# The last block's output path: VectorE 32x32 turns and 128-byte rows for five of six chunks, in place of TensorE turns

## The chip, the cores and the metric

The kernel runs on one core of one Trainium2 chip. The metric is the device time of one execution in microseconds (us), the median of several runs.

## The reference

Sigmoid attention over 4 batches, 12 heads, 448 tokens and head size 64 gives 1792 rows of 768 columns. Two mixture-of-experts layers follow. The first sends a token through its expert only where a skip score is above zero, and adds its result to the token. The second sends every token through the expert with the highest cosine score. Only the second matters here:

```python
h = np.maximum(x[mask] @ w1[e], 0.0)      # 768 -> 1024
out[mask] = gate_w[mask, None] * (h @ w2[e])   # 1024 -> 768, scaled per token
```

The output is float32, 1792 x 768, in token order.

## The kernel before

The kernel works on one batch of 448 tokens at a time, and holds activations turned: 128 of the 768 columns on the partitions, 448 tokens along the free axis. In the second layer each batch has one expert that most of its tokens chose. That expert runs densely over the whole batch ("block", `dense`). The few tokens with another expert are gathered into an "item" of 32 places, run through their own expert, and scattered to the output by row number with an indirect DMA on GpSimd's queue.

There are four such blocks, j = 0 to 3, in an order that the routing sets at run time. A block loops over f = 0 to 7 (128 hidden units each). `h(f)` makes hidden units with 18 matmuls (every product is three matmuls, from operands split into a high and a low part), and `y(f - 1)` adds the previous units' share to six PSUM tiles `YS[0]` to `YS[5]`, one per chunk of 128 output columns, 18 matmuls again. Hooks `sub(0)` to `sub(15)` between them run small steps of other work at fixed places. The order of instructions on each engine is the order in which the code writes them. Waits between engines, and between DMAs and engines, are put in by the framework from the tiles and tensors that an instruction reads and writes, unless the code declares two instructions independent (`declare_no_dep`).

The result of a block is in PSUM with columns on the partitions, and the output wants tokens on rows, so it has to be turned and scaled by each token's gate.

Blocks 0 to 2 do it in `finish`. VectorE turns each chunk in squares of 32x32 (L1421) from PSUM into the tile `STG`; the access pattern places token 14r + k at column 32k + r beforehand, so that partition 32g + r then holds the tokens 14r to 14r + 13, and of each chunk the 32 columns of group g. GpSimd multiplies by the gate (L1423) into the tile `ROW`; the gate comes in that layout from `gate_tokens`, which makes it in two steps among the hooks: a VectorE product (L1403) and one small matmul (L1410) with a copy (L1412). Four DMAs on SyncE's queue (L1430) then store it, one for each group g of 32 partitions, in rows of 32 floats, 128 bytes. These stores are issued at hook 2 of the next block.

The last block does it in `finish_last`, because no later block hides it. Its last two steps f = 6 and 7 are ordered chunk by chunk. ScalarE or VectorE copies a finished chunk to `STG` (L1450, L1448, and for the last chunk half each, L1445 and L1446). TensorE transposes it in four pieces of 112 tokens (L1394) into PSUM places that have come free. ScalarE (L1467) and VectorE (L1465) scale a token row each by the gate, which lies on the partitions here. Three stores (L1470) follow: chunks 0 to 2 on SyncE's queue, chunks 3 and 4 on ScalarE's queue, chunk 5 on SyncE's. Between the second store and the work for chunk 5 comes `it.early`: the item's second product into `YS[0]`, 64 matmuls (L1031), its gate (L1045) and its scatter (L1068).

The stores of `finish_last` are declared independent of each other only where they are on different queues:

```python
for other in STORES:
    if other.ins.engine != st.ins.engine:
        tc.declare_no_dep(st.ins, other.ins, reason="disjoint columns")
```

The four stores of `finish` have no such declaration.

Of the kernel before, what the change touches and what calls it, by code (L numbers as in the profile page):

```python
# [14 lines left out]
ALU = mybir.AluOpType  # L15
# [6 lines left out]
def sigmoid_attention_moe_moe_kernel(  # L22
# [1359 lines left out]
    e = expert_of(0)  # L1382
    b = nc.values_load(K["pb"][0:1, 8:9], engines=[ENG.SP], min_val=0, max_val=B - 1)

    def scaled(g, c, d, n, t):
        row = ROW[:P, c * DM + d * 128 : c * DM + (d + n) * 128]
        if (c + (n == 2)) % 2:
            nc.vector.tensor_scalar(row, t, g[:, c : c + 1], None, op0=ALU.mult)
        else:
            nc.scalar.activation(row, t, AF.Copy, scale=g[:, c : c + 1])  # L1390

    def turn_out(t, w, c, d):
        o = d * S + c * P
        nc.tensor.transpose(t[:P, w : w + 128], STG[:, o : o + P], ident)  # L1394

    def gate_tokens(j, box):

        a = SEL[:P, :128]

        def ready():  # L1400
            g = dense_gate(R2, j)
            four = [P, 4, C, 8]
            nc.vector.tensor_tensor(  # L1403
                a.rearrange("p (g c r) -> p g c r", g=4, r=8), g.unsqueeze(1).unsqueeze(3).to_broadcast(four),
                K["seg"][:P].unsqueeze(1).unsqueeze(1).to_broadcast(four), op=ALU.mult,
            )

        def turned():
            ps = bank("ps_gt")
            nc.tensor.matmul(ps[:, :NK], lhsT=a, rhs=K["off"][:P], start=True, stop=True)  # L1410
            t = box["gt"] = sm.tile([128, NK], F32, tag="gtt", name="gtt", bufs=1)
            nc.vector.tensor_copy(t, ps[:, :NK])  # L1412

        return {3: ready, 8 if j else 9: turned}

    def finish(j, b, gt):

        turned = STG.rearrange("p (d k f) -> p d k f", d=ND, f=32)
        ready = ROW[:, : ND * S].rearrange("p (k d f) -> p k d f", d=ND, f=32)
        for d in range(ND):  # L1420
            nc.vector.transpose(turned[:, d], YS[d][:, :S].rearrange("p (r k) -> p k r", k=NK))  # L1421
        for d in range(ND):
            nc.gpsimd.tensor_tensor(  # L1423
                ready[:, :, d], turned[:, d], gt.unsqueeze(2).to_broadcast([128, NK, 32]), op=ALU.mult
            )

        def store():
            to = out.rearrange("(b r k) (d g f) -> b r k d g f", b=B, k=NK, g=4, f=32)
            for g in range(4):
                nc.sync.dma_start(  # L1430
                    to[ds(b, 1), :, :, :, g].rearrange("o r k d f -> r (o k) d f"), ready[32 * g : 32 * g + 32]
                )

        return store

    def finish_last(j, b, it=None):


        place = {0: BANKS + YS[1:3], 3: YS[3:5] + BANKS, 5: [YS[1], YS[2]]}

        def copy(c):
            o = STG[:, c * S : (c + 1) * S]
            if c == ND - 1:
                w = S // 2
                nc.scalar.activation(o[:, :w], YS[c][:, :w], AF.Copy)  # L1445
                nc.vector.tensor_copy(o[:, w:], YS[c][:, w:S])  # L1446
            elif c % 2:
                nc.vector.tensor_copy(o, YS[c][:, :S])  # L1448
            else:
                nc.scalar.activation(o, YS[c][:, :S], AF.Copy)  # L1450

        def turns(d, d0):
            for c in range(C):
                if d0 < 5:
                    turn_out(place[d0][c], (d - d0) * 128, c, d)
                else:
                    turn_out(place[d0][c % 2], c // 2 * 128, c, d)

        def store(g, d0, d1, queue, bq):
            for c in range(C):  # L1460
                row = ROW[:P, c * DM + d0 * 128 : c * DM + d1 * 128]
                n = (d1 - d0) * 128
                t = place[d0][c][:P, :n] if d0 < 5 else place[d0][c % 2][:P, c // 2 * 128 : c // 2 * 128 + 128]
                if c % 2:
                    nc.vector.tensor_scalar(row, t, g[:, c : c + 1], None, op0=ALU.mult)  # L1465
                else:
                    nc.scalar.activation(row, t, AF.Copy, scale=g[:, c : c + 1])  # L1467
            cols = slice(d0 * 128, d1 * 128)
            to = out.rearrange("(b c p) d -> p b c d", c=C, p=P)[:, ds(bq, 1), :, cols]
            st = queue.dma_start(  # L1470
                to.rearrange("p o c d -> p (o c) d"),
                ROW[:P].rearrange("p (c d) -> p c d", d=DM)[:, :, cols],
            )
            for other in STORES:
                if other.ins.engine != st.ins.engine:
                    tc.declare_no_dep(st.ins, other.ins, reason="disjoint columns")
            STORES.append(st)

        def end(yc, rest):
            g = dense_gate(R2, j)  # L1480
            bq = batch_of(j)

            def both(c):
                yc(NF - 2, c)
                yc(NF - 1, c)
                copy(c)

            for c in range(3):
                yc(NF - 2, c)
            rest()  # L1490
            for c in range(3):
                yc(NF - 1, c)
                copy(c)
            both(3)
            for d in range(3):
                turns(d, 0)
            store(g, 0, 3, nc.sync, b)
            both(4)
            turns(3, 3)
            turns(4, 3)  # L1500
            store(g, 3, 5, nc.scalar, bq)
            early = it.early(STORES) if it else None
            both(5)
            turns(5, 5)
            store(g, 5, 6, nc.sync, b)
            if early:
                tc.declare_no_dep(STORES[-1].ins, early, reason="rows of another batch")
                it.late(STORES)

        return end  # L1510
# [7 lines left out]
    for j in range(B):  # L1518
        box = {"e": e}
        last = j == B - 1  # L1520
        if last:
            todo = {}
        else:
            todo = at_subs((3, 5, 7), route2_steps(j + 1, XST[(j + 1) % 2])[:3])
            for n, at in ROUTED.get(j, ()):
                todo = merge(todo, at_subs(at, route2_steps(n, None)[3:]))
            todo = merge(todo, gate_tokens(j, box))
        if j == 0:
            load_unit(v1, v2, e, 1)
            halves()  # L1530
            for f in split_unit(0, FIRST_RAW)[3:]:
                f()
            todo = merge({-0.5: lambda: spread(item_b())}, todo)
        if j == B - 2:
            todo = merge(todo, item_steps(R2, (9, 11, 13)), {13: lambda: likely("single")})
        if pend:
            todo = merge({2: pend}, todo)

        def units2(k):
            u, r = k // 4, k % 4  # L1540
            if r == 0 and u + 2 < NU:
                load_unit(v1, v2, box["e"], u + 2)
            if k == 10 and not last:
                box["n"] = expert_of(j + 1)
                load_unit(v1, v2, box["n"], 0)
            if (u + 1 < NU or not last) and r % 2 == 0:
                for f in split_unit((u + 1) % NU)[:3] if r == 0 else split_unit((u + 1) % NU)[3:]:
                    f()
            if k == 12 and not last:
                load_unit(v1, v2, box["n"], 1)  # L1550

        xs = XST[j % 2]
        if not last:
            dense(xs, beside(units2, todo))
            pend = finish(j, b, box["gt"])
            b, e = nc.values_load(K["pb"][0:1, 9 + j : 10 + j], engines=[ENG.SP], min_val=0, max_val=B - 1), box["n"]
            continue

        def with_item():
            it = Item(1, 0)  # L1560
            at, prep = it.ready(0)
            steps = schedule(merge(todo, at), prep, (5, 5, 7))
            dense(xs, beside(units2, steps), end=finish_last(j, b, it))

        n = 3 * NL[1]
        with tc.If(nc.values_load(R2.LI[0:1, n + 3 : n + 4], min_val=0, max_val=NL[1]) < 1, label="single") as cmp:
            with tc.If(count(R2) > 0) as cmp2:
                with_item()
            with cmp2.Else():
                STORES = []  # L1570
                dense(xs, beside(units2, todo), end=finish_last(j, b))
            with tc.If(nc.values_load(R2.LI[0:1, n + 1 : n + 2], min_val=0, max_val=NL[1]) > 0):
                others(1)
        with cmp.Else():
            STORES = []
            with_item()
# [33 lines left out]
```

## Time and profile before

| | |
|---|---|
| time, median of 3 runs | 552.51 us (551.93 to 552.78) |
| the profiled execution's own time | 553.05 us |
| its span, first to last instruction | 551.2 us |
| TensorE matmul busy | 542.9 us, 98% of the span |
| VectorE busy | 298.4 us, 54% |
| ScalarE busy | 252.4 us, 46% |
| GpSimd busy | 54.8 us, 10% |
| mean granted TensorE clock | 0.999 |

Busy time is an engine's time in instructions, and the span is what the profiler recorded between the first and the last instruction. The profiled execution is one run with its own time, some tenths from the median of the three. Times in the rows below are microseconds from the start of the span, and a duration in ns is marked as such.

### The profile page before, as it was taken

Reading aid. Unit: us, or ns where it says so; the run is one execution under the profiler, and the core shown is the slowest. Engines: PE = TensorE matmul, PEld = TensorE weight load, DVE = VectorE, ACT = ScalarE, POOL = GpSimd, SP = SyncE. Lnnn points to the kernel's source line nnn. Section 1 sums busy time; section 2 is a strip of 40 time slices with the busy share of each in tenths; the row PEclk is TensorE's granted clock in tenths of the full one; section 3 lists DMA queues with packets and bytes.
Section 4 is the critical chain, followed back from the end, with each engine's and each line's share of the span. In section 5 each row is a group of like instructions: output and inputs, shape, how many; then the busy total and the mean of one; then the engine's idle time right before and its main releaser. Section 6 shows DMA issues by size and latency. Waiting matters only on the chain.

```text
span 551.2 us, 10110 instructions
## 1 busy us (share of the span) xinstructions
PE 542.9 (98%) x3663; PEld 425.3 (77%) x3663; DVE 298.4 (54%) x810; ACT 252.4 (46%) x410; POOL 54.8 (10%) x133
## 2 busy tenths in 40 slices
PE   8999999999999999999999999999999999999995
PEld 5464644645389889899869898999899998989984
DVE  3643445237777678674138777694486435543212
ACT  5766676766943365323209462175233421222112
POOL 5010000000000000254000000040003000305000
PEclk9999999999999999999999999999999999999999
DMA  9777666773561513315637106227624731546353
GB/s 179 138 124 135 115 111 112 126 129 83 200 187 50 172 58 120 115 59 160 242 121 283 55 15 241 89 48 171 213 76 103 219 118 59 141 81 226 115 226 105
DMA packets 169712, 73.34 MB, mean 133 GB/s; under 512 B 134466, under 2 KB 161302, under 8 KB 169632
## 3 DMA queue, kind: packets, MB, share of 16 engines
q1 hardware_dynamic: 147904, 65.94, 44.4%
q10 hardware_dynamic: 21360, 5.97, 4.5%
q0 software_dynamic: 368, 0.53, 0.5%
q8 instruction: 31, 0.51, 0.4%
q14 instruction: 49, 0.40, 0.2%
HBM read 66.90 MB, written 5.60 MB: 132 GB/s over the span
## 4 chain that ended last, share of the span: by engine, by line
PE 96%; DVE 1%; ACT 1%; issue 0%; DVEq 0%; POOL 0%; POOLq 0%; ACTq 0%
PE psS L622 11%; PE bank L814 11%; PE y L814 11%; PE psO L640 11%; PE bank L816 11%; PE y L816 11%; PE y L815 11%; PE bank L815 11%; PE bank L1006 1%; PE y L1031 1%; PE bank L250 1%; PE busy L658 1%; PE ps_r L250 1%; ACT A L626 1%; PE ps_t L598 0%; PE y L1394 0%
## 5 line engine op out<-in xcount | busy, mean ns | idle before, releaser
L834 ACT ACTIVATE hh<-bank 128x448 fp32r<-128x448 f32 x48 | 26.1, 545 | 191.1 <-PE bank L816 175.6
L814 PE MATMUL y<-hh,h 128*128 128x448 f32 x288 | 107.3, 372 | 0.0
L814 PE MATMUL bank<-xs,h 128*128 128x448 f32 x288 | 107.0, 372 | 0.0
L816 PE MATMUL bank<-xs,l 128*128 128x448 f32 x288 | 105.4, 366 | 0.2 <-DVE l L805 0.2
L816 PE MATMUL y<-hh,l 128*128 128x448 f32 x288 | 105.5, 366 | 0.0
L815 PE MATMUL y<-hl,h 128*128 128x448 f32 x288 | 105.5, 366 | 0.0
L815 PE MATMUL bank<-xs,h 128*128 128x448 f32 x288 | 105.3, 366 | 0.0
L626 ACT ACTIVATE A<-psS,bias 128x896 f32<-128x896 f32 x84 | 83.3, 1006 | 34.7 <-PE psS L622 34.4
L835 DVE SCALAR_TENSOR_TENSOR hl<-bank,hh 128x448 fp32r<-128x448 f32 x48 | 29.9, 622 | 121.1 <-ACT hh L834 117.8
L805 DVE TENSOR_TENSOR l<-r,h 128x512 fp32r<-128x512 f32 (+1 forms) x115 | 87.4, 810 | 4.4 <-ACT h L804 2.7
L622 PE MATMUL psS<-qT,kT 64*64 64x448 f32 x672 | 87.4, 541 | 0.4 <-ACT A L626 0.3
L640 PE MATMUL psO<-A,v 64*64 64x448 f32 x672 | 86.6, 539 | 0.0
L804 ACT ACTIVATE h<-r 128x512 fp32r<-128x512 f32 (+1 forms) x115 | 74.3, 709 | 1.2 <-DMA r<-in_moe_w_dram 1.1
L814 PEld LDWEIGHTS bank<-xs,h 128*128 128x128 f32 x288 | 54.1, 188 | 8.5 <-issue 1.6
L640 PEld LDWEIGHTS psO<-A,v 64*64 64x64 f32 x672 | 34.7, 133 | 32.5 <-issue 19.8
L814 PEld LDWEIGHTS y<-hh,h 128*128 128x128 f32 x288 | 54.1, 188 | 5.6 <-issue 1.2
L816 PEld LDWEIGHTS bank<-xs,l 128*128 128x128 f32 x288 | 54.1, 188 | 5.1 <-DVE l L805 0.6
L815 PEld LDWEIGHTS y<-hl,h 128*128 128x128 f32 x288 | 54.1, 188 | 4.7 <-issue 0.2
L816 PEld LDWEIGHTS y<-hh,l 128*128 128x128 f32 x288 | 54.1, 188 | 4.7
L815 PEld LDWEIGHTS bank<-xs,h 128*128 128x128 f32 x288 | 54.1, 188 | 4.3
L622 PEld LDWEIGHTS psS<-qT,kT 64*64 64x64 f32 x672 | 32.3, 132 | 30.8 <-issue 15.8
L982 POOL COPY row<-xT 128x6 f32 x64 | 18.4, 307 | 209.4 <-DVE row L973 197.8
(271 smaller groups left out, 421.0 us busy)
## 6 DMA issues: line engine op xcount, KB each, us to landing
r<-in_moe_w_dram SPq DMA_DIRECT2D x62, 768.0 KB, 5.0
k<-in_k_dram SPq DMA_DIRECT2D x44, 112.0 KB, 2.8
q<-in_q_dram SPq DMA_DIRECT2D x44, 112.0 KB, 3.5
v<-in_v_dram ACTq DMA_DIRECT2D x44, 112.0 KB, 2.9
out_dram<-row SPq DMA_DIRECT2D x12, 336.0 KB, 3.8
stg<-in_moe_w_dram SPq DMA_DIRECT2D x1, 768.0 KB, 7.5
row<-in_moe_w_dram SPq DMA_DIRECT2D x1, 768.0 KB, 8.7
out_dram<-row SPq DMA_DIRECT2D x1, 672.0 KB, 3.9
```

Of the source, the lines that this page charges most:

```text
L250: nc.tensor.matmul(ps[q : q + 32, :w], lhsT=lhsT, rhs=tokens(rhs, h), start=first, stop=last)
L622: nc.tensor.matmul(ps[KT * i : KT * i + KT, j, :S], lhsT=kT[r, i, h * KT : (h + 1) * KT], rhs=qT[r, i], start=True, stop=True,)
L626: nc.scalar.activation(at, ps[:, :, :S], AF.Sigmoid, bias=bias, scale=1.0 / math.sqrt(D))
L640: nc.tensor.matmul(ST[w, "o"][i][D * j : D * j + D, :S], lhsT=t[r, j, h, :], rhs=at[r, j, :], start=h == 0, stop=h == NH - 1,)
L804: nc.scalar.activation(dst_h, src, AF.Copy)
L805: nc.vector.tensor_sub(dst_l, src, dst_h.bitcast(F32))
L814: nc.tensor.matmul(ps, lhsT=ah, rhs=bh, start=first, stop=False)
L815: nc.tensor.matmul(ps, lhsT=ah, rhs=bl, start=False, stop=False)
L816: nc.tensor.matmul(ps, lhsT=al, rhs=bh, start=False, stop=last)
L834: nc.scalar.activation(a, ps[:, :S], AF.Relu)
L835: nc.vector.scalar_tensor_tensor(l, ps[:, :S], 0.0, a.bitcast(F32), op0=ALU.max, op1=ALU.subtract)
L982: nc.gpsimd.tensor_copy(self.xb[:, :, t : t + 1], xT[:, :, ds(o, 1)])
```

## The change

In the last block, chunks 0 to 4 go the way of `finish`. Each is turned by VectorE as soon as it is complete and gated by GpSimd (chunks 0 and 2) or VectorE (1, 3 and 4). Then four DMAs on SyncE's queue store the five chunks in 128-byte rows. Chunk 5 keeps TensorE's transposes, after one copy by ScalarE, and its store stays on SyncE's queue, behind the four. The last block therefore gets `gate_tokens` too, at hooks 2 and 4, with a tile from `spare()` in place of `SEL`. No store is left on ScalarE's queue, and the loop with `declare_no_dep` between stores is gone; the one between chunk 5's store and the item's scatter stays.

```diff
+    def turned_chunk(d):
+        nc.vector.transpose(TURNED[:, d], YS[d][:, :S].rearrange("p (r k) -> p k r", k=NK))
+
+    def gated_chunk(d, n, gt, engine):
+        engine.tensor_tensor(
+            ready(n)[:, :, d], TURNED[:, d], gt.unsqueeze(2).to_broadcast([128, NK, 32]), op=ALU.mult
+        )
+
+    def store_chunks(b, n):
+        to = out.rearrange("(b r k) (d g f) -> b r k d g f", b=B, k=NK, g=4, f=32)
+        return [
+            nc.sync.dma_start(
+                to[ds(b, 1), :, :, :n, g].rearrange("o r k d f -> r (o k) d f"),
+                ready(n)[32 * g : 32 * g + 32],
+            )
+            for g in range(4)
+        ]
...
+        d = ND - 1
+        last = ROW[:P, d * S : d * S + C * 128]
+        place = (YS[1], YS[2])
+
+        def chunk(yc, c, *fs):
+            for f in fs:
+                yc(f, c)
+            turned_chunk(c)
+            gated_chunk(c, d, box["gt"], nc.gpsimd if c in (0, 2) else nc.vector)
+
+        def last_chunk(g):
+            o = STG[:, d * S : d * S + S]
+            nc.scalar.activation(o, YS[d][:, :S], AF.Copy)
             for c in range(C):
+                t = place[c % 2][:P, c // 2 * 128 : c // 2 * 128 + 128]
+                nc.tensor.transpose(t, o[:, c * P : c * P + P], ident)
...
             for c in range(3):
-                yc(NF - 1, c)
-                copy(c)
-            both(3)
-            for d in range(3):
-                turns(d, 0)
-            store(g, 0, 3, nc.sync, b)
-            both(4)
-            turns(3, 3)
-            turns(4, 3)
-            store(g, 3, 5, nc.scalar, bq)
+                chunk(yc, c, NF - 1)
+            for c in range(3, d):
+                chunk(yc, c, NF - 2, NF - 1)
+            STORES.extend(store_chunks(b, d))
             early = it.early(STORES) if it else None
-            both(5)
-            turns(5, 5)
-            store(g, 5, 6, nc.sync, b)
+            yc(NF - 2, d)
+            yc(NF - 1, d)
+            STORES.append(last_chunk(g))
             if early:
                 tc.declare_no_dep(STORES[-1].ins, early, reason="rows of another batch")
                 it.late(STORES)
...
-            todo = {}
+            todo = gate_tokens(j, box)
```

## Rows read from the trace of the kernel before

**Rows 1.** The page: the chain that ended last, by engine.

```profile
PE 96%; DVE 1%; ACT 1%; issue 0%; DVEq 0%; POOL 0%; POOLq 0%; ACTq 0%
```

**Rows 2.** The chain in the tail: start, length, engine, tile, line.

```profile
536.99 0.22 PE bank L1394 x2
...
538.30 0.20 PE y L814
...
539.53 0.02 issue
...
541.13 2.74 PE y L1031 x64
...
545.31 0.02 issue
...
546.70 0.35 DVE row L1465
```

**Rows 3.** Timeline, SyncE's queue, tail: the last store.

```profile
547.47 0.35 SPq L1470 DMA_DIRECT2D out_dram<-row  x1
```

**Rows 4.** DMA issues, 539 to 548 us: queue, KB, median us to landing.

```profile
out_dram<-row SPq DMA_DIRECT2D x1, 672.0 KB, 3.9
out_dram<-row ACTq DMA_DIRECT2D x1, 448.0 KB, 3.3
out_dram<-row SPq DMA_DIRECT2D x1, 224.0 KB, 2.4
```

**Rows 5.** Timeline, SyncE's queue: stores two to four after block 1.

```profile
423.00 0.59 SPq L1430 DMA_DIRECT2D out_dram<-row  x1
...
426.74 0.58 SPq L1430 DMA_DIRECT2D out_dram<-row  x1
...
430.47 0.58 SPq L1430 DMA_DIRECT2D out_dram<-row  x1
```

**Rows 6.** SyncE's queue, 418 to 432 us: waits in total, times, longest.

```profile
SPq L1430 <- DMA out_dram<-row: 8.9, 3, 3.0
```

**Rows 7.** Line L1430: landing after issue, all 12 stores.

```profile
DMA to landing us min/median/max: 3.7/3.8/5.4
```

**Rows 8.** Timeline, SyncE's queue: the item's four weight loads.

```profile
528.05 2.25 SPq L936 DMA_DIRECT2D r<-in_moe_w_dram  x4
```

**Rows 9.** Windows, the store of 423.00 us and the last one: last columns DMA share, GB/s.

```profile
424.25:424.50 0.25, 0.25 (x3) 0.23 (x2) 0.18 (x1) 0.25 (x2) 0.00 (x0) 1.00 0.97 163
424.50:424.75 0.25, 0.25 (x3) 0.24 (x2) 0.21 (x1) 0.25 (x2) 0.00 (x0) 1.00 1.21 207
426.00:426.25 0.25, 0.25 (x3) 0.23 (x2) 0.25 (x1) 0.17 (x1) 0.00 (x0) 1.00 0.10 15
...
548.75:549.00 0.25, 0.00 (x0) 0.00 (x0) 0.00 (x0) 0.00 (x0) 0.00 (x0) 1.00 1.06 309
549.25:549.50 0.25, 0.00 (x0) 0.00 (x0) 0.00 (x0) 0.00 (x0) 0.00 (x0) 1.00 0.21 59
```

**Rows 10.** Timeline of the tail: the copies that follow chunks 0 and 3.

```profile
534.65 0.55 ACT L1450 ACTIVATE stg<-y 128x448 f32<-128x448 f32 x1 [2.11 <-PE y L816]
...
537.03 0.62 DVE L1448 COPY stg<-y 128x448 f32<-128x448 f32 x1 [1.20 <-PE y L816]
```

**Rows 11.** Groups by line and form: busy us, mean ns of one.

```profile
L1421 DVE STREAM_TRANSPOSE stg<-y 128x448 f32<-128x448 f32 x18 | 10.7, 636 | 1.1 <-PE y L816 1.1
L735 DVE TENSOR_TENSOR xg<-xT,G 128x448 f32<-128x448 f32 x12 | 7.4, 622 | 1.9 <-ACT G L725 1.7
L1423 POOL TENSOR_TENSOR row<-stg,gtt 128x448 f32<-128x448 f32 x18 | 17.2, 992 | 202.8 <-DVE stg L1421 202.8
```

**Rows 12.** Line L1423: ns min/median/max.

```profile
L1423 POOL TENSOR_TENSOR row<-stg,gtt x18: 937/942/1391, 357.8 to 478.4; 128x448 f32<-128x448 f32 x18
```

**Rows 13.** Timeline, TensorE, around block 1's gate matmul.

```profile
445.03 0.29 PE L1410 MATMUL bank<-off,sel 112*128 112x14 f32 x2
...
445.46 0.36 PE L815 MATMUL y<-hl,h 128*128 128x448 f32 x1
```

More of the change, by code (lines that the diff above doesn't have):

```diff
@@ L1383, in sigmoid_attention_moe_moe_kernel @@
     b = nc.values_load(K["pb"][0:1, 8:9], engines=[ENG.SP], min_val=0, max_val=B - 1)
[L1385 to L1394, printed above, removed]
     def gate_tokens(j, box):
-        a = SEL[:P, :128]
+        a = (SEL if j < B - 1 else spare())[:P, :128]
         def ready():
@@ L1412, in turned @@
             nc.vector.tensor_copy(t, ps[:, :NK])
-        return {3: ready, 8 if j else 9: turned}
+        return {2: ready, 4: turned} if j == B - 1 else {3: ready, 8 if j else 9: turned}
+    TURNED = STG.rearrange("p (d k f) -> p d k f", d=ND, f=32)
+    ready = lambda n: ROW[:, : n * S].rearrange("p (k d f) -> p k d f", d=n, f=32)
+    def turned_chunk(d):
[4 more added lines that the diff above has]
+        )
@@ L1416, in finish @@
+    def store_chunks(b, n):
[7 more added lines that the diff above has]
+        ]
     def finish(j, b, gt):
-        turned = STG.rearrange("p (d k f) -> p d k f", d=ND, f=32)
-        ready = ROW[:, : ND * S].rearrange("p (k d f) -> p k d f", d=ND, f=32)
@@ L1420, in finish @@
         for d in range(ND):
-            nc.vector.transpose(turned[:, d], YS[d][:, :S].rearrange("p (r k) -> p k r", k=NK))
+            turned_chunk(d)
         for d in range(ND):
[L1423 to L1452, printed above, removed]
-            for c in range(C):
[L1454 to L1459, printed above, removed]
+            gated_chunk(d, ND, gt, nc.gpsimd)
@@ new lines, in finish, with finish_last @@
+        return lambda: store_chunks(b, ND)
+    def finish_last(j, b, box, it=None):
+        d = ND - 1
[9 more added lines that the diff above has]
+            nc.scalar.activation(o, YS[d][:, :S], AF.Copy)
+            for c in range(C):
+                t = place[c % 2][:P, c // 2 * 128 : c // 2 * 128 + 128]
+                nc.tensor.transpose(t, o[:, c * P : c * P + P], ident)
@@ L1460, in store @@
             for c in range(C):
-                row = ROW[:P, c * DM + d0 * 128 : c * DM + d1 * 128]
-                n = (d1 - d0) * 128
-                t = place[d0][c][:P, :n] if d0 < 5 else place[d0][c % 2][:P, c // 2 * 128 : c // 2 * 128 + 128]
+                t = place[c % 2][:P, c // 2 * 128 : c // 2 * 128 + 128]
+                row = last[:, c * 128 : c * 128 + 128]
                 if c % 2:
@@ L1467, in store @@
                     nc.scalar.activation(row, t, AF.Copy, scale=g[:, c : c + 1])
[L1468 to L1477, printed above, removed]
+            to = out.rearrange("(b c p) d -> p b c d", c=C, p=P)[:, ds(b, 1), :, d * 128 :]
+            return nc.sync.dma_start(to.rearrange("p o c d -> p (o c) d"), last.rearrange("p (c d) -> p c d", c=C))
         def end(yc, rest):
             g = dense_gate(R2, j)
-            bq = batch_of(j)
-            def both(c):
-                yc(NF - 2, c)
-                yc(NF - 1, c)
-                copy(c)
             for c in range(3):
@@ L1491, in end @@
             for c in range(3):
-                yc(NF - 1, c)
-                copy(c)
-            both(3)
-            for d in range(3):
-                turns(d, 0)
-            store(g, 0, 3, nc.sync, b)
-            both(4)
-            turns(3, 3)
-            turns(4, 3)
-            store(g, 3, 5, nc.scalar, bq)
+                chunk(yc, c, NF - 1)
+            for c in range(3, d):
+                chunk(yc, c, NF - 2, NF - 1)
+            STORES.extend(store_chunks(b, d))
             early = it.early(STORES) if it else None
-            both(5)
-            turns(5, 5)
-            store(g, 5, 6, nc.sync, b)
+            yc(NF - 2, d)
+            yc(NF - 1, d)
+            STORES.append(last_chunk(g))
             if early:
@@ L1562, in with_item @@
             steps = schedule(merge(todo, at), prep, (5, 5, 7))
-            dense(xs, beside(units2, steps), end=finish_last(j, b, it))
+            dense(xs, beside(units2, steps), end=finish_last(j, b, box, it))
         n = 3 * NL[1]
@@ L1570, in sigmoid_attention_moe_moe_kernel @@
                 STORES = []
-                dense(xs, beside(units2, todo), end=finish_last(j, b))
+                dense(xs, beside(units2, todo), end=finish_last(j, b, box))
             with tc.If(nc.values_load(R2.LI[0:1, n + 1 : n + 2], min_val=0, max_val=NL[1]) > 0):
```

## The prediction

> **What bounds the kernel now.** I read the page's chain first: TensorE holds 96% of it [rows 1]. The change touches only the end of the last block, so the next view is the same chain from 537 us on [rows 2]. There the reader sees two stretches that are not products. The transposes of chunks 0 to 2 run from 536.99 to 538.30 us, 1.31 us. The transposes of chunks 3 and 4, with the wait for the copy ahead of them, run from 539.53 to 541.13 us, 1.60 us. After them come the item's product (2.74 us) and chunk 5, whose matmuls end at 545.31 us; copy, transposes and scaling take until the last store is issued at 547.47 us [rows 3]. It lands 2.4 us later [rows 4], at 549.87 us, and the span of 551.2 us ends 1.33 us after that. So the last landing sets the end, and what counts is when the last store can be issued.
>
> Then I read SyncE's queue, since the change moves its stores to the form that blocks 0 to 2 use. There the four stores of a block are not issued one behind the other. After block 1 the second to fourth start at 423.00, 426.74 and 430.47 us, 3.74 and 3.73 us apart [rows 5]. The list of waits says why: SyncE waited 3 times, 8.9 us in all, for the DMA of an earlier store [rows 6], and the landing of such a store takes at least 3.7 us, 3.8 at the median [rows 7], the very gap. The queue itself allows closer issue: four weight loads, which go to tiles of their own, were issued within 2.25 us [rows 8]. So each store waits until the one before has landed, a dependence through the output tensor. In blocks 0 to 2 it costs nothing, because half a block of matmuls follows. At the end of the kernel nothing follows.
>
> **The change part by part.**
>
> *TensorE's turns removed.* Five chunks of four transposes, with their stalls, are the 1.31 + 1.60 = 2.91 us above. The item's product and chunk 5 move forward by that.
>
> *Gate in the new layout.* Around the same small matmul in block 1 TensorE goes from 445.03 to 445.46 us for it and one product [rows 13]; a product alone is paced at 0.20 us [rows 2], so it costs 0.23 us. Its VectorE steps at hooks 2 and 4 lie under half a block of matmuls: nothing, and if a hook found VectorE late, the matmul two hooks on would cover it. Net, TensorE is done 2.91 - 0.23 = 2.68 us earlier, at 542.63 us. Chunk 5's single copy against two halves is worth some tenths more; with about 2 us for copy, transposes and scaling (2.16 now), its data are ready near 544.6 us. That gain decides only if the store may be issued then.
>
> *VectorE's turns and gates.* Chunk 0 is ready at 534.65 and chunk 3 at 537.03 us [rows 10]; chunk 4 follows six products later, near 538.25. A turn is 0.636 us and a multiply of this size on VectorE 0.622 us (the nearest row, with both inputs and the output in SBUF) [rows 11]. Five turns and three gates on VectorE are 5 x 0.636 + 3 x 0.622 = 5.05 us from 534.65, so they end at 539.70 us; by TensorE alone it would be 538.25 + 0.636 + 0.622 = 539.51. Add 0.23 us for the gate matmul: 539.93. GpSimd's two gates at 0.99 us (up to 1.39) [rows 11, 12] follow the turns of chunks 0 and 2 and end by 539 us, inside VectorE's chain. I put the first store at 539.95 us. Lower bound 539.75. Upper bound: the five gated chunks interleave in `ROW`, 32 columns at a time; if gates on different engines are made to wait for each other there, VectorE's gate 1 waits for GpSimd's gate 0 and gate 3 for gate 2, about 0.75 us for the first (1.39 us slowest) and 0.4 for the second, 1.2 us in all.
>
> *The four stores.* Each carries 32 partitions x 14 tokens x 5 chunks x 128 bytes = 286,720 bytes against 344,064 now. A store of today starts moving data some 1.25 us after issue and moves at about 205 GB/s, 1.7 us [rows 9]. At that rate 57,344 bytes less save 0.28 us: 3.73 - 0.28 = 3.45 us from issue to landing. Bounds: 3.73 (nothing saved) and 5/6 of 3.73, 3.11 (all of it in proportion). Nothing else moves data at that time but the item's scatter, so I leave out the 5.4 us that one store took [rows 7].
>
> *The last store.* It stands behind the four on SyncE's queue and writes the same batch of the output. No code declares it independent of them, so I take it that it too waits for the fourth to land. It has today's size and form, 2.4 us [rows 4]. What waits behind it is the end of the program.
>
> *Sum.* 539.95 + 4 x 3.45 = 553.75 us for the issue of the last store, against 547.47: 6.3 us later. Its data have then been ready for some 9 us, so all of TensorE's gain is lost in this wait. Span 551.2 + 6.3 = 557.5; the execution's own time 553.05 + 6.3 = 559.35. The profiled execution was 0.54 us above the median of the three runs, so the median after is 552.51 + 6.3 = **558.8 us**, 1.1% slower.
>
> The Trainium skill (DMA: Bandwidth & Descriptors, "Anatomy of one DMA — SWDGE (gpsimd) path") fits one DMA of GpSimd's kind as 2.0 us plus its bytes at 436 GB/s; as an estimate from that page a store of 286,720 bytes would take 2.66 us and the sum would be 3.2 us lower, near 555.6 us. It would give 2.79 us for today's store, which measures 3.73 here on SyncE's queue [rows 5], so the measurement decides.
>
> **The rivals.**
>
> *A: the stores do not wait for each other.* Then the change is faster. The four are issued in about 2.4 us, and 4 x 286,720 bytes at 205 GB/s take 5.6 us, from 539.95 + 1.25 to 546.8 us. Chunk 5's bytes queue behind them: 229,376 bytes at about 300 GB/s [rows 9] are 0.76 us, and the landing comes some 0.45 us after the last byte (549.4 to 549.87 now). Landing 548.0 instead of 549.87: 1.9 us faster, 550.6 us. For it: the columns and rows are disjoint. Against it: they are just as disjoint in blocks 0 to 2, and there the wait is in the trace each time [rows 5, 6]. The point where it decides is (547.47 - 539.95) / 4 = 1.9 us per store; below that the chain is shorter than the old path.
>
> The Trainium skill (the same page, "Specifications") asks for at least 512 bytes per transfer piece for the full rate; the trace agrees, 207 GB/s with 128-byte rows and 309 with 512-byte rows [rows 9]. By it rival A gains less than its issue times promise, as reckoned there.
>
> *B: the four wait, but the last store does not.* It is issued 0.58 us behind the fourth, at 550.9 us. The fourth's bytes end near 550.3 + 1.25 + 1.4 = 552.95, chunk 5's at 553.7, and it lands near 554.2: 4.3 us later than now, 556.8 us. For it: its columns are a block of their own. Against it: the store pieces of blocks 0 to 2 were also disjoint.
>
> *C: the gates wait across engines in `ROW`*, 1.2 us on top of the forecast: 560.0 us. For it: interleaved destinations. Against it: each gate writes columns of its own, and no row of before shows two engines writing such a pattern.
>
> **How the numbers follow.** Forecast 0.70, B 0.11, C 0.11, A 0.08. The lowest of the slow cases is B at 556.8; the forecast with 3.11 us per store and the early first store is 558.8 - 1.36 - 0.2 = 557.2. The highest is C with 3.73 us per store, 560.0 + 1.1 = 561.1. I give 556.6 to 561.0, which leaves out A. A change of under 0.2%, 1.1 us, could not be told from none: A lies beyond that at -1.9 us, with a part for a smaller gain. Faster 0.07, same 0.01, slower 0.92.
>
> **What would show it.** In the profile after, SyncE's five stores of the last block should start about 3.45 us apart, the list of waits should name the output's DMA ahead of four of them, and TensorE should finish near 542.6 us with four transposes and nothing else to do for some 14 us. L1394 should show 4 transposes instead of 24. I am wrong if the five stores start 0.6 us apart (A), if the fifth follows the fourth at once (B), or if VectorE waits for GpSimd between gates (C). A landing far from 3.45 us would move the sum by four times the error.

## The result, and the profile after

The changed kernel takes 558.96 us (median of 4 runs, 558.84 to 559.69) against 552.37 us (4 runs of the kernel before, its first three and one more). The ratio is 1.0124, 95% interval 1.0111 to 1.0136: 6.6 us slower. The forecast was 558.8 us.

The profiled execution has a span of 557.1 us and took 558.99 us. In it the last block reaches its end part some 0.65 us earlier than in the profile of before: VectorE's first turn starts at 534.00 us, where the first copy stood at 534.65 [rows 10]. That is the spread of the code ahead of it, not the change: in a run of the kernel before with one store moved (below), the first store of the tail came 0.97 us earlier than in the profile of before. So intervals are compared here, not clock times. The first turn:

```profile
534.00 0.65 DVE L1410 STREAM_TRANSPOSE stg<-y 128x448 f32<-128x448 f32 x1 [0.53 <-PE y L816]
```

SyncE's queue in the tail, in order of time: start, length, line.

```profile
539.56 0.69 SPq L1422 DMA_DIRECT2D out_dram<-row  x1
...
543.06 0.60 SPq L1422 DMA_DIRECT2D out_dram<-row  x1
...
546.47 0.60 SPq L1422 DMA_DIRECT2D out_dram<-row  x1
...
549.89 0.60 SPq L1422 DMA_DIRECT2D out_dram<-row  x1
...
553.48 0.39 SPq L1464 DMA_DIRECT2D out_dram<-row  x1
```

Five stores, 3.50, 3.41, 3.42 and 3.59 us apart. The same queue's waits from 530 us on (total, times, longest) and the landings (KB, median us) say what each step is:

```profile
SPq L1422 <- DVE row L1414: 9.2, 1, 9.2
SPq L1422 <- DMA out_dram<-row: 7.9, 3, 2.6
SPq L1464 <- DMA out_dram<-row: 2.7, 1, 2.7
```

```profile
out_dram<-row SPq DMA_DIRECT2D x4, 280.0 KB, 3.4
out_dram<-row SPq DMA_DIRECT2D x1, 224.0 KB, 2.3
```

The first store waits for VectorE's last gate. The next three and chunk 5's store wait for the landing ahead, each for the rest of the 3.4 us that a landing takes. This is the pattern of [rows 5] and [rows 6], now at the end of the program.

The chain of waits on the compute engines shows when chunk 5 was ready. TensorE's last product ends at 541.77 us, and VectorE's first scaling starts at 543.14. The timeline has its second, the last piece of chunk 5, at 543.41, so the data are complete at 543.75. That chain ends there: it holds none of the stores, though the span goes on to 557.1 us, so the end of this program is read from SyncE's queue.

```profile
541.77 0.02 issue
...
541.86 0.55 ACT stg L1452
...
543.14 0.35 DVE row L1460
```

```profile
543.41 0.34 DVE L1460 TENSOR_SCALAR row<-y,dg 112x128 f32<-112x128 f32 x1
```

The store of these data starts at 553.48 us. They lie ready for 9.7 us, which is more than everything that TensorE had gained.

From the first turn (copy, before) to the issue of the last store it was 547.47 - 534.65 = 12.8 us; it is now 553.48 - 534.00 = 19.5 us. The difference, 6.7 us, agrees with the 6.6 us of the medians.

### The profile page after: what moved, and what is told of

Its sections match the earlier page's. It is cut to its first block, busy times and chain, and to the rows that moved or that the text cites. A ratio compares the mean times of both kernels' runs of the same rounds, so it can differ in the third digit from the quotient of the medians.

```text
span 557.1 us, 10069 instructions
## 1 busy us (share of the span) xinstructions
PE 539.6 (97%) x3645; PEld 422.7 (76%) x3645; DVE 301.0 (54%) x816; ACT 248.8 (45%) x403; POOL 56.0 (10%) x135
## 4 chain that ended last, share of the span: by engine, by line
PE 94%; DVE 1%; ACT 1%; DMA 1%; issue 0%; DVEq 0%; ACTq 0%
PE psS L622 11%; PE bank L814 11%; PE y L814 11%; PE psO L640 11%; PE bank L816 11%; PE y L816 11%; PE y L815 11%; PE bank L815 10%; PE bank L1006 1%; PE y L1031 1%; PE bank L250 1%; DMA k<-in_k_dram 1%; PE ps_r L250 1%; ACT A L626 1%; PE ps_t L598 0%
## 5 line engine op out<-in xcount | busy, mean ns | idle before, releaser
L1414 POOL TENSOR_TENSOR row<-stg,gtt 128x448 f32<-128x448 f32 x20 | 19.1, 986 | 228.8 <-DVE stg L1410 228.8
```

What stands on the lines that cost most here:

```text
L1414: engine.tensor_tensor(ready(n)[:, :, d], TURNED[:, d], gt.unsqueeze(2).to_broadcast([128, NK, 32]), op=ALU.mult)
```

## The experiments

The theory: the loss is a chain of landings, made by stores on one queue that each depend on the one before through the output tensor. The rivals: TensorE or VectorE still sets the end; the queue or the 128-byte rows would hold the stores apart without any dependence; only the last store's wait matters.

### No dependence between the stores

```diff
+    SCR = [nc.dram_tensor(f"scr{g}", [NT, DM], F32).ap() for g in range(4)]
...
+        to = [view(t) for t in (SCR if n < ND else [out] * 4)]
...
-                to[ds(b, 1), :, :, :n, g].rearrange("o r k d f -> r (o k) d f"),
+                to[g][ds(b, 1), :, :, :n, g].rearrange("o r k d f -> r (o k) d f"),
```

> The changed kernel, with the four stores of the last block each going to a DRAM tensor of its own, so that chunks 0 to 4 of that block are not in the output; chunk 5's store still goes to the output. Issue order, sizes, row length and queue stay. Theory (the stores wait for each other's landing through the output tensor): the five stores start about 0.6 us apart, the first four within 2.5 us of 539.6 us and the last when its data are ready, near 543.5; their bytes queue at about 205 GB/s until 546.4 us, the last lands near 547.6, the span ends near 549 us and the time is about 550.8 us, 8 us under the changed kernel and 1.5 under the kernel before. Rival (the queue itself, or 128-byte rows, hold the stores 3.4 us apart): the starts stay 3.4 us apart and the time stays at 559 us.

Measured: 552.41 us, ratio to the kernel before 0.9997 (0.9988 to 1.0006). The 6.6 us are gone: with a tensor for each store the time is that of the kernel before, so the waits through the output tensor make the loss. The gain of 1.5 us that the theory promised did not come. SyncE's queue:

```profile
539.77 0.68 SPq L1425 DMA_DIRECT2D scr<-row  x1
...
540.69 0.94 SPq L1425 DMA_DIRECT2D scr<-row  x1
...
541.82 1.96 SPq L1425 DMA_DIRECT2D scr<-row  x1
...
543.97 1.24 SPq L1425 DMA_DIRECT2D scr<-row  x1
...
545.47 1.25 SPq L1467 DMA_DIRECT2D out_dram<-row  x1
```

No store waits for a landing any more (none is listed ahead of them). Yet the issuing instruction itself grows from 0.68 to as much as 1.96 us once two stores are under way. The last store starts at 545.47 us though its data were scaled by 543.96, and takes 3.6 us to land behind the others' bytes. This resembles the rival, in a weaker form: it cannot make the loss, but it eats the gain. What lengthens the issue is not shown. A run with the four stores on one queue into the output itself, declared independent there, was not made.

### The same with long rows

As above, but each store writes 32 contiguous pieces (the lines that differ; the rest of the function is left out):

```diff
...
+                    SCR[g].rearrange("n d -> (n d)").rearrange("(b r x) -> b r x", b=B, r=32)[ds(b, 1), :, : n * S]
+                    .rearrange("o r x -> r (o x)"),
+                    ROW[32 * g : 32 * g + 32, : n * S],
...
```

> As the run with own tensors (no wait between the stores; chunks 0 to 4 of the last block are not in the output), but each of the four stores writes 32 contiguous pieces of 8,960 bytes instead of 2,240 rows of 128 bytes. Same bytes, queue and issue points. Theory (what was left there, no gain over the kernel before, is the price of 128-byte rows: the queue takes the next store only as its rows drain, 0.9 to 2.0 us of issue each): issues fall to 0.3 to 0.7 us, the bytes move at about 300 GB/s, the last store starts near 543.6 us and lands near 546.2; the time is about 549.3 us, 3 us below the kernel before. Rival (the queue holds back any fifth store, whatever its rows): issues stay above 1 us and the time near 552.4 us.

Measured: 550.82 us, ratio 0.9969 (0.9958 to 0.9980). Half of each guess holds:

```profile
540.09 0.39 SPq L1424 DMA_DIRECT2D scr<-row  x1
...
540.69 0.34 SPq L1424 DMA_DIRECT2D scr<-row  x1
...
541.13 0.55 SPq L1424 DMA_DIRECT2D scr<-row  x1
...
541.77 1.31 SPq L1424 DMA_DIRECT2D scr<-row  x1
...
544.36 0.33 SPq L1475 DMA_DIRECT2D out_dram<-row  x1
```

Issue falls to 0.3 to 0.6 us, but the fourth store still takes 1.31 us. The last store is no longer held: its data were scaled by 544.23 us. It lands only after 4.0 us, because earlier bytes are still moving; they went at 90 to 358 GB/s in half-microsecond windows, not at a steady 300. So short rows cost 1.6 us here by the medians (552.41 against 550.82), and 1.0 us by the two traces, from the first turn to the last landing (14.9 against 13.9 us). And four or five large stores close together cost more than their issue times say, whatever the rows.

### Only the last store set free

```diff
-            return nc.sync.dma_start(to.rearrange("p o c d -> p (o c) d"), last.rearrange("p (c d) -> p c d", c=C))
+            return nc.scalar.dma_start(to.rearrange("p o c d -> p (o c) d"), last.rearrange("p (c d) -> p c d", c=C))
...
+            for other in STORES[:-1]:
+                tc.declare_no_dep(STORES[-1].ins, other.ins, reason="disjoint columns")
```

> The changed kernel, with chunk 5's store alone on ScalarE's queue and declared independent of the four. Theory (four separate waits in a chain of five): the last store starts near 543.6 us as soon as its data are ready, the four keep their 3.4 us steps, and the fourth's landing near 553.3 us sets the end; the time falls by the one step that went, 2.5 us, to about 556.5 us. Rival (what costs is only that the last store waits): the time falls by the whole 6 to 8 us to about 551 us.

Measured: 557.75 us, ratio 1.0093 (1.0078 to 1.0108), 1.2 us under the changed kernel instead of the 2.5 expected. ScalarE's queue issues the last store as soon as its data are ready; SyncE's steps are 3.5, 4.5 and 3.4 us:

```profile
543.73 0.38 ACTq L1464 DMA_DIRECT2D out_dram<-row  x1
```

```profile
539.40 0.71 SPq L1422 DMA_DIRECT2D out_dram<-row  x1
...
542.92 0.60 SPq L1422 DMA_DIRECT2D out_dram<-row  x1
...
547.42 0.60 SPq L1422 DMA_DIRECT2D out_dram<-row  x1
...
550.83 0.60 SPq L1422 DMA_DIRECT2D out_dram<-row  x1
```

The step in which both queues have bytes under way is the long one, by 1.1 us; that accounts for most of what is missing from the 2.5 us. The three waits that are left make most of the loss; it is not the last wait alone.

### The kernel before, all stores on one queue

```diff
-            store(g, 3, 5, nc.scalar, bq)
+            store(g, 3, 5, nc.sync, b)
```

> The kernel before, with the store of chunks 3 and 4 moved from ScalarE's queue to SyncE's, so that its three stores are in one chain as well. Theory (a wait costs only where the data are ready before the landing ahead): the second store waits until the first has landed at 543.4 us instead of starting at 542.0 and lands near 546.7, still ahead of the last store's 547.5 us; no change, within 0.1%. Rival (a second store queue is worth something by itself, in issue time or in bytes moved): slower by 0.5 us or more.

Measured: 552.21 us, ratio 0.9996 (0.9987 to 1.0005). The second store does wait, and it costs nothing:

```profile
538.48 0.38 SPq L1470 DMA_DIRECT2D out_dram<-row  x1
...
542.51 0.35 SPq L1470 DMA_DIRECT2D out_dram<-row  x1
...
546.45 0.32 SPq L1470 DMA_DIRECT2D out_dram<-row  x1
```

```profile
SPq L1470 <- DMA out_dram<-row: 3.4, 1, 3.4
```

The gap to the second is 4.03 us, a landing (3.9 us, [rows 4]); the third store's data are ready after the second has landed. The same dependence is free with two such gaps to fill and costly with four back to back. Nor is a second queue worth anything by itself here.

### TensorE's gain given back

```diff
             STORES.extend(store_chunks(b, d))
+            for _ in range(26):
+                nc.tensor.transpose(BANKS[0][:, :128], ident, ident)
```

> The changed kernel, with 26 more TensorE transposes of the identity into a PSUM bank that nobody reads, between chunk 4's products and the item's product, about 2.9 us: TensorE's gain from the change is given back. Theory (TensorE's gain is lost in the wait of the last store, whose data are ready some 10 us early): TensorE ends near 544.7 us instead of 541.8 and the time stays at 559.0 us within 0.1%. Rival (TensorE still sets the end in part): slower by up to 2.9 us, about 562 us.

Measured: 559.52 us, ratio 1.0123 (1.0107 to 1.0138), where the changed kernel's is 1.0124. The median is 0.56 us above the changed kernel's 558.96, but the runs of the two overlap, and the ratios agree. The 26 transposes took 3.0 us, and the last copy starts at 544.93 instead of 541.86 us; the last store starts 14.00 us after the first, against 13.92:

```profile
537.67 3.00 PE L1477 MATMUL bank<-ident 128*128 128x128 f32 x26
```

```profile
539.80 0.69 SPq L1422 DMA_DIRECT2D out_dram<-row  x1
...
553.80 0.39 SPq L1464 DMA_DIRECT2D out_dram<-row  x1
```

Three more microseconds of TensorE cost nothing that can be measured: its gain was lost in the wait.

### All gates on VectorE

```diff
-            gated_chunk(c, d, box["gt"], nc.gpsimd if c in (0, 2) else nc.vector)
+            gated_chunk(c, d, box["gt"], nc.vector)
```

> The changed kernel, with the gates of chunks 0 and 2 on VectorE instead of GpSimd, so that GpSimd is idle there. Theory (VectorE's gates of chunks 1 and 3 took 0.86 and 0.94 us because GpSimd worked beside them, chunk 4's 0.62 alone): all five gates take 0.62 us; VectorE then has 5 x 0.64 + 5 x 0.62 = 6.3 us from 534.0, the first store starts near 540.2 us instead of 539.6, and the end and the time move by the same 0.6 to 0.7 us, to 559.6. Rival (the longer gates come from PSUM or the store's layout): gates 1 and 3 stay near 0.9 us, and the first store starts near 540.8.

Measured: 560.12 us, ratio 1.0139 (1.0123 to 1.0154). Every gate takes 0.62 or 0.63 us with GpSimd idle, two of them here:

```profile
535.92 0.62 DVE L1414 TENSOR_TENSOR row<-stg,gtt 128x448 f32<-128x448 f32 x1
...
538.36 0.63 DVE L1414 TENSOR_TENSOR row<-stg,gtt 128x448 f32<-128x448 f32 x1
```

The first store starts at 540.23 and the last at 554.15 us, both 0.67 us later than in the changed kernel, as the theory has it:

```profile
540.23 0.69 SPq L1422 DMA_DIRECT2D out_dram<-row  x1
...
554.15 0.39 SPq L1464 DMA_DIRECT2D out_dram<-row  x1
```

So VectorE's chain sets where the row of landings begins, one for one. The medians differ by 1.2 us, more than that, and the runs of the two do not overlap (558.84 to 559.69 against 559.96 to 560.50), only the intervals of the ratios do. In the traces the span is 1.07 us longer: 0.67 us from the gates, and 0.40 us behind the last landing, for which no run gives a cause.

### Two versions of the kernel

If TensorE and the tail set the end before, their order there should be worth something by itself:

```diff
-            if c == ND - 1:
-                w = S // 2
-                nc.scalar.activation(o[:, :w], YS[c][:, :w], AF.Copy)
-                nc.vector.tensor_copy(o[:, w:], YS[c][:, w:S])
-            elif c % 2:
+            if c % 2 and c < ND - 1:
...
             both(4)
+            early = it.early(STORES) if it else None
             turns(3, 3)
             turns(4, 3)
             store(g, 3, 5, nc.scalar, bq)
-            early = it.early(STORES) if it else None
+            if early:
+                tc.declare_no_dep(STORES[-1].ins, early, reason="rows of another batch")
```

> The kernel before, with TensorE's turns kept and two things reordered: the item's product stands ahead of the turns of chunks 3 and 4, so that TensorE does not wait 0.6 us for the copy of chunk 4, and chunk 5 is copied by ScalarE in one piece, as in the changed kernel. Theory (in the old path TensorE and the tail behind it set the end): 0.6 us less on TensorE and 0.3 us less in the tail, about 0.9 us faster than the kernel before, 551.6 us. Rival (the later store of chunks 3 and 4, issued near 543.5 instead of 542.0 us, or ScalarE's fuller order, takes it back): no change.

Measured: 551.95 us, ratio 0.9990 (0.9981 to 0.9999): faster, by 0.6 us of the 0.9 expected, and the interval only just leaves out no change. From the first copy to the issue of the last store the trace shows 12.07 us, where the kernel before takes 12.82. All of that 0.75 us is TensorE's order. The copy in one piece, put at 0.3 us, brings nothing: from its start to VectorE's first scaling it takes 1.29 us, where the two halves took 1.30. The kernel before, then this run:

```profile
545.40 0.36 ACT stg L1445
...
545.81 0.87 PE y L1394 x4
...
546.70 0.35 DVE row L1465
```

```profile
543.12 0.38 ACTq L1466
...
543.61 0.55 ACT stg L1446
...
544.21 0.66 PE y L1394 x4
...
544.90 0.35 DVE row L1461
```

The rival's part is small: the store of chunks 3 and 4 now stands on ScalarE ahead of the copy, which starts 0.54 us after the start of TensorE's last product instead of 0.47.

The other takes from the change what is good in it: VectorE's turns for the three chunks that are ready first, and their four stores on three queues: two on SyncE, one each on ScalarE and GpSimd. It keeps the order of the run above, the item's product ahead of the turns of chunks 3 and 4.

```diff
...
+            store_group(nc.sync, b, 0)
+            store_group(nc.scalar, bq, 1)
+            store_group(nc.gpsimd, bp, 2)
...
+            if it:
+                EARLY.append(it.early([st for st in STORES if st.ins.engine != STORES[2].ins.engine]))
+            store_group(nc.sync, b, 3)
+            turns(3)
+            turns(4)
+            store(g, 3, 5, nc.scalar, bq)
```

> VectorE's turns for chunks 0 to 2 alone; their four 128-byte stores go to SyncE (two), ScalarE and GpSimd, declared independent across queues; chunks 3 to 5 keep TensorE's turns and the old two stores, with the item's product ahead of the turns. Only two stores of this block then wait for a landing on their own queue, with data to spare. Theory (the change's loss is the chain of landings at the end; spread over queues and started 2 us earlier it is off the path): the last store starts near 544.5 to 545 us and the time is about 550.4 us, 2 us faster than the kernel before. Rival (128-byte rows on three queues still take their 205 GB/s, and GpSimd's own descriptors are slow): the last store is held until 546 us or later, 552 us or more.

Measured: 550.20 us, ratio 0.9960 (0.9946 to 0.9973): 2.4 us faster than the kernel before, 8.8 us faster than the changed one. SyncE and GpSimd:

```profile
536.89 0.71 SPq L1454 DMA_DIRECT2D out_dram<-row  x1
...
540.22 0.60 SPq L1454 DMA_DIRECT2D out_dram<-row  x1
...
544.38 0.39 SPq L1477 DMA_DIRECT2D out_dram<-row  x1
```

```profile
537.51 1.43 POOL L1454 DMA_DIRECT2D out_dram<-row  x1 [1.28 <-issue]
543.00 1.10 POOL L1068 DMA_INDIRECT out_dram<-xg,small  x1 [4.06 <-DMA out_dram<-row]
```

The waits for landings are still there: SyncE's second store starts 3.33 us after the first, and the item's scatter waits 4.06 us for GpSimd's store. None is the last thing any more. The last store starts within 0.15 us of its data (scaled by 544.26 us). From the first turn to its issue it is 10.72 us, 2.10 less than the 12.82 of the kernel before: 0.75 is the order of the run above, and the rest agrees with the 1.31 us of TensorE's turns of chunks 0 to 2, which are gone. So the gain is TensorE's time, set free because no landing holds the end. That it takes three queues, an early start or both is not shown: no run has these four stores on one queue.

## Why the prediction was right, by its steps

*The waits.* Right, and shown: they are in the trace four times, and in the run with a tensor for each store, which has none of them, the loss is gone. The step from issue to issue was put at 3.45 us, from the landing of a 336 KB store less 0.28 us for its fewer bytes; it measured 3.41 to 3.59 us, 13.92 us in all against 13.80. The last store waited like the others, so rival B did not occur.

*The first store.* Put at 5.07 us after the first turn's start (539.95 against 534.65 and 0.23 for the gate matmul); it measured 5.56 us. Two gates on VectorE were mis-sized. The price of 0.622 us came from rows with GpSimd idle; beside GpSimd's gates two of the three took longer:

```profile
534.73 0.94 POOL L1414 TENSOR_TENSOR row<-stg,gtt 128x448 f32<-128x448 f32 x1 [24.84 <-DVE stg L1410]
536.79 0.94 POOL L1414 TENSOR_TENSOR row<-stg,gtt 128x448 f32<-128x448 f32 x1 [1.12 <-DVE stg L1410]
```

```profile
535.29 0.86 DVE L1414 TENSOR_TENSOR row<-stg,gtt 128x448 f32<-128x448 f32 x1
...
537.27 0.94 DVE L1414 TENSOR_TENSOR row<-stg,gtt 128x448 f32<-128x448 f32 x1
...
538.80 0.62 DVE L1414 TENSOR_TENSOR row<-stg,gtt 128x448 f32<-128x448 f32 x1
```

By the prediction's own sign for rival C, VectorE waiting for GpSimd between gates, a part of C occurred: 0.56 us in the two gates, against C's 1.2. Its mechanism did not. VectorE's gate starts while GpSimd's is still running, so no wait was put in for its destination in `ROW`; the instruction itself takes longer.

*The sum.* The change was put at 6.3 us and is 6.6. The first store is 0.49 us later than forecast and the four steps are 0.12 us longer. Against them stand the 0.23 us of the gate matmul, which lies ahead of the first turn and cannot be told from the spread there, and an end that comes 0.16 us sooner after the last issue. That the forecast of 558.8 us lies still closer to the measured 558.96 is in part luck: the forecast starts from 552.51 us, and with one more run the kernel before has a median of 552.37.

*TensorE.* Its last product was put at 542.63 us, 7.75 us after the first turn; it came at 7.77. Chunk 5's single copy, "worth some tenths more", is worth 0.02 us (1.28 us from the copy's start to VectorE's first scaling, 1.30 before). That the gain is worth nothing is shown by the run with 26 more transposes.

*Rival A.* It did not occur, and it was sized wrong: 550.6 us, where the run without dependence took 552.4. Two of its terms failed. "The four are issued in about 2.4 us", taken from four weight loads and from single stores, left out that a store's issue grows when others are under way: there it took 5.4 us, from 539.77 to 545.21. And the bytes of all five stores, put at 5.6 + 0.76 = 6.4 us, took about 7.5, which makes most of the difference:

```profile
541.00:541.50 0.50, 0.50 (x4) 0.47 (x3) 0.04 (x1) 0.00 (x0) 0.17 (x1) 1.00 0.83 142
...
548.00:548.50 0.50, 0.00 (x0) 0.00 (x0) 0.00 (x0) 0.00 (x0) 0.00 (x0) 0.50 0.73 207
```

The rates of 207 and 309 GB/s that the prediction sets side by side for short and long rows come from stores of 32 and 112 partitions, so they do not show the row length alone. The two runs without dependence do, with 32 partitions each: the first store landed 2.8 us after issue with long rows and 3.5 us with short ones.

## What to carry to other kernels

Before a piece of code is reused at another place, read what hides its waits where it stands now: four stores, each waiting 3.4 to 3.7 us for the one before, lie ahead of half a block of matmuls in blocks 0 to 2 (no run tests that they are free there), and at the end of the program their kind cost 6.6 us. At a tail, count the steps from issue to landing in series on each queue, not bytes or engine time; a gain on the busiest engine is worth nothing behind them, and counts again once they are off the end. What was off the end here were stores of one tensor on different queues, declared independent and started as early as their data allowed.

## What the runs showed of the hardware that was not expected

Issuing a store is not a fixed cost. On SyncE's queue one store of 2,240 rows of 128 bytes took 0.68 us to issue alone, and up to 1.96 us with two others under way; with 32 pieces of 8,960 bytes it took 0.34 to 0.55 us, and the fourth 1.31. No run shows what holds the issue.

VectorE's multiply of two SBUF tiles hardly runs beside GpSimd's: both delayed gates end 0.48 us after GpSimd's gate does (536.15 against 535.67, 538.21 against 537.73), whenever they began, and alone such a gate takes 0.62 us. In the run with GpSimd idle none was delayed, and the turns, which read PSUM, took no longer beside GpSimd's gate (0.60 to 0.65 us) than with GpSimd idle (0.64 or 0.65). In the run with three queues the one gate on VectorE took 1.15 us and again ended 0.48 us after GpSimd's (536.71 against 536.23). The Trainium skill (SBUF — State Buffer, "SBUF: two separate sides") states that the two engines share one pair of ports under an exclusive lock, which a VectorE instruction with two SBUF inputs needs against a GpSimd instruction that reads SBUF, and that the later one waits for the whole of the other. The trace agrees, with the 0.48 us that are left each time after GpSimd's end.
